# Attention of block 1 spread over the second pair of QKV quads, its regroup and output projection moved into the next FFN1

## The chip, the cores and the metric

The kernel runs on one core of a Trainium2 chip. The core has a matrix engine (TensorE, PE in the profile), three engines that work on vectors (VectorE or DVE, ScalarE or ACT, GpSimd or POOL), a queue engine (SyncE, SP), and 16 DMA engines that are fed from queues of SP, ACT and POOL. Each engine runs its own instructions strictly in the order in which the program lists them; an instruction that waits holds up all behind it on its engine. The metric is the device time of one execution in microseconds.

## The reference

The input x has 2048 tokens of 576 channels. It is normalised per token, and two branches are added to it:

```
xn  = layernorm(x)
q, k, v = split(xn @ wqkv)          # 32 heads of 18 channels
A: for token t: the 8 keys at t, t-2, ..., t-14 (those before token 0 are masked)
   o[t] = sum_w softmax_w(q[t].k[t-2w] / sqrt(18)) v[t-2w];   A = o @ wo
B: h = relu(xn @ w1 + b1) ** 2      # 576 -> 4608
   B = h @ w2 + b2                  # 4608 -> 576
out = x + A + B
```

## The kernel before

The tokens are worked on in four blocks of 512 (b = 0..3), two blocks making a half s. All products run on PE with operands split into a high and a low part of type fp32r, three partial products for each. ACT makes the high part (an activation), DVE the low part (a subtraction). So each weight tile costs PE its matmuls, ACT one instruction and DVE one, ahead of time: `w2_hi`/`w2_lo` split the FFN2 and projection weights two tiles ahead in the order of the list `stream`, in three buffers `w2s`; a buffer is loaded from memory three tiles ahead (`load_w2`, issued at the end of `w2_lo`).

The stages follow one another on PE:

1. q0: QKV of blocks 0 and 1, row by row.
2. `phase_a(0)`: FFN1 of blocks 0 and 1 in 18 pairs of hidden tiles (`ffn_pair`, a Strassen-like scheme over 2 x 2 parts, lines 524 to 649), with FFN2 of block 0 and then its output projection filled in between; the hidden tiles of block 1 go to memory.
3. `phase_b0` (945): FFN2 of block 1 in 36 steps n, then QKV of blocks 2 and 3 in four units of 14 quad steps each (`quad_step`, 890), then the output projection of block 1.
4. `phase_a(1)`: FFN1 of blocks 2 and 3, with FFN2 and the projection of block 2.
5. `phase_b1` (1094): FFN2 and the projection of block 3 in 34 + 5 steps, and `tail`.

The quads also follow a Strassen-like scheme. There are two pairs of units: k = 0 makes the channel groups 0 and 1, k = 1 the groups 2 and 3; half = 0, 1 are the two units of a pair. A unit has the steps (s, i) in the order (1,0) (1,1) (2,0) (2,1) (3,0) (3,1) (5,0) (4,0) (5,1) (4,1) (7,0) (6,0) (7,1) (6,1); s names the product, i one of two sets of four PSUM banks. This text counts the units 0 to 3 and the steps of a unit n = 0 to 13. Steps 0 to 5 have 6 matmuls each, steps 6 to 13 have 8. Steps with s = 4 to 7 send a row of results away through `row` (908): ACT copies the bank into one of four buffers `st` and, for s = 4 and 6, DVE adds a second bank (line 95, `st<-p,st`). Step (6,i) accumulates in the bank that the add of step (4,i) reads. After each step `hook` (986) issues work for other stages, mostly the splitting of weights.

Attention does not use PE. A block has four groups of heads (order 3, 2, 1, 0 for block 1). `attention(b, g)` (361) is a generator: up to each `yield` it issues one piece, and a group has 18 pieces: for j = 0..3 a product of queries with shifted keys (`pr<-q,kv`) and a reduction (`lg<-pr`); one piece with the maximum, its subtraction and the exponential on ACT (`lg<-lg`, line 380); one with the sum, reciprocal and scaling; for j = 0..3 a product with the values (`pr<-lg,kv`) and a tree of three additions (`pr<-pr` twice, `q<-pr`). After the last piece POOL issues 8 DMAs of the result to memory (`o<-q`, 400).

`side(k)` issues the next k pieces from the queue of groups; called with False it stops in front of a piece marked "exp". `complete(b)` issues all that is left of the blocks up to b at once. Keys and values have three buffers `kv`; `free` counts the free ones, `release` (348) gives one back and calls `fetch` (332), which loads the next keys or values on POOL's DMA queue. `regroup(1, .)` (706) takes such a buffer as well, and reads block 1's attention output back in two DMAs (`kv<-o`, 713). `o_hi(b, c)` and `o_lo(b, c)` (724, 743) transpose a fifth of it on DVE and split it (ACT, DVE) for the output projection `add(b, o_ops(b, c))`; the last one (c = 4) gives the buffer back.

Before the change `hook` calls `complete(1)` and `regroup(1, 0)` after the last step of unit 1 and then offers two groups of block 2. During units 2 and 3 pieces of group (2, 0) are issued, `o_hi` and `o_lo` for c = 0..3 follow steps 8 and 13 of unit 3, the projection parts c = 0, 1, 2 stand between the quads and FFN1, and c = 3, 4 are issued by `filler` inside the first pair of FFN1 at its places 0 and 1 (`work(0)`, `work(1)`). Temporary tiles of the name "r4" come from a pool of four buffers (`four`, 114).

Of the kernel before, what the change touches and what calls it, by code (L numbers as in the profile page):

```python
# [21 lines left out]
NJ = TB // P  # L22
# [23 lines left out]
def block_kernel(ctx: ExitStack, tc: tile.TileContext, x, xt, wqkv, wo, w1, b1, w2, b2, out):  # L46
# [280 lines left out]
        a = t[:, j:j + 1, 0:1]  # L327
        return bass.AP(tensor=a.tensor, offset=a.offset, ap=[a.ap[0], [DIL * CG, W], *dims])

    loads, landed, queue, free, lane, held = [], {}, [], [0], [nc.sync], [False]  # L330

    def fetch():
        while free[0] and loads and not held[0]:
            free[0] -= 1
            kind, b, g = loads.pop(0)
            if kind == "x":
                load_rows(b)
                landed["x", b] = True
                continue
            t = landed[kind, b, g] = sb.tile([P, NE, CG], F32, name="kv", bufs=3)  # L340
            if kind == "k":
                q = landed["q", b, g] = sb.tile([P, NJ, CG], F32, name="q", bufs=2)
                lane[0].dma_start(q.rearrange("p j c -> p (j c)"),
                                  flat(scr["q"][g], (PAD + b * TB) * CG, [NJ * CG, P], NJ * CG))
            lane[0].dma_start(t.rearrange("p e c -> p (e c)"),
                              flat(scr[kind][g], (PAD + b * TB - HALO) * CG, [NJ * CG, P], NE * CG))
# [14 lines left out]
    def attention(b, g):  # L361
        k, q = landed.pop(("k", b, g)), landed.pop(("q", b, g))
        lg = sb.tile([P, NA, W], F32, name="lg")
        mx = sb.tile([P, NA], F32, name="mx")
        sm = sb.tile([P, NA], F32, name="sm")
        for j in range(NJ):
            pr = sb.tile([P, W, CG], F32, name="pr")
            tt(pr, q[:, j:j + 1].to_broadcast([P, W, CG]), shifted(k, j, [1, CG]), ALU.mult)
            if j == NJ - 1:
                release()  # L370
            yield
            nc.vector.tensor_reduce(out=lg[:, j * HG:(j + 1) * HG].rearrange("p a w -> p w a"),  # L372
                                    in_=pr.rearrange("p w (a d) -> p w a d", d=DH), axis=AX.X, op=ALU.add)
            yield "exp" if j == NJ - 1 else None
        if b == 0:
            l4 = lg[:4].rearrange("p (j h) w -> p j h w", j=NJ)
            tt(l4, l4, mask[:4, :, None].to_broadcast([4, NJ, HG, W]), ALU.add)
        nc.vector.tensor_reduce(out=mx, in_=lg, axis=AX.X, op=ALU.max)
        tt(lg, lg, mx[:, :, None].to_broadcast([P, NA, W]), ALU.subtract)
        nc.scalar.activation(lg, lg, AF.Exp, scale=SCALE)  # L380
        yield
        nc.vector.tensor_reduce(out=sm, in_=lg, axis=AX.X, op=ALU.add)
        nc.vector.reciprocal(sm, sm)
        tt(lg, lg, sm[:, :, None].to_broadcast([P, NA, W]), ALU.mult)
        yield
        v = landed.pop(("v", b, g))
        for j in range(NJ):
            pr = sb.tile([P, W, CG], F32, name="pr")
            at = lg[:, j * HG:(j + 1) * HG].rearrange("p a w -> p w a")
            tt(pr.rearrange("p w (a d) -> p w a d", d=DH), at[:, :, :, None].to_broadcast([P, W, HG, DH]),  # L390
               shifted(v, j, [DH, HG], [1, DH]), ALU.mult)
            yield
            tt(pr[:, :4], pr[:, :4], pr[:, 4:], ALU.add)
            tt(pr[:, :2], pr[:, :2], pr[:, 2:4], ALU.add)
            tt(q[:, j], pr[:, 0], pr[:, 1], ALU.add)
            if j == NJ - 1:
                for k, (a, z) in enumerate(OPART):
                    rows = oscr[b, k][g * L:(g + 1) * L].rearrange("l (j i) c -> l i j c", i=G)
                    for i in range(G):
                        nc.gpsimd.dma_start(rows[:, i], q[i * L:(i + 1) * L, :, a:z])  # L400
                release()
            yield
# [3 lines left out]
    def side(k, exp=True):  # L406
# [13 lines left out]
                current[0] = None  # L420
        return 0

    def complete(b):
        while (any(n[0] == "k" and n[1] <= b for n, _ in queue)
               or current[0] is not None and current[2][0] == "k" and current[2][1] <= b):
            left = side(1)
            assert not left or current[0] is None

# [95 lines left out]
    def ffn_pair(s, p, work, first=False):  # L524
# [55 lines left out]
        if not last:  # L580
            combine_w1(n + 1)
        if not first:
            side(1 if p == 1 else 2 + p % 2, False)
        work(0)
        product(bb, T2, ss(2))
        w2_hi()
# [119 lines left out]
    def regroup(b, k):  # L706
        if b == 1:
            assert free[0]
            free[0] -= 1
            t = sb.tile([P, NJ * G * CG], F32, name="kv", bufs=3)  # L710
            for i, n in enumerate((OA, OB)):
                ob[b, i] = t[:, i * NJ * G * OA:][:, :NJ * G * n].rearrange("p (r c) -> p r c", c=n)
# [232 lines left out]
    def phase_b0():  # L945
# [6 lines left out]
        for n in range(NF):  # L952
# [7 lines left out]
            if n % 2 and n // 2 + 3 < NP:  # L960
                load_h(0, n // 2 + 3)
            if n < 33:
                run(pieces, 1 + n % 2)
            if n == 3:
                load_xt(3)
            if n == 33:
# [19 lines left out]
        def hook(k, half, s, i):  # L986
# [9 lines left out]
            if half and not k:  # L996
# [32 lines left out]
                if (s, i) == (6, 1):  # L1029
                    split_side(1, 1)  # L1030
                    split_slot(B22, b22)
                    complete(1)
                    regroup(b, 0)
                    for g in (0, 1):
                        offer(2, g)
            if at == (1, 0, 2, 1):
# [2 lines left out]
            if half and k:  # L1039
# [3 lines left out]
                    w1_hi(NP, 0)  # L1043
                    w1_lo(NP, 0)
                if (s, i) == (5, 1):
                    o_hi(b, 0), o_hi(b, 1)
                    o_lo(b, 0), o_lo(b, 1)
                if (s, i) == (4, 1):
                    w1_hi(NP, 1)
                    w1_lo(NP, 1)  # L1050
                if (s, i) == (6, 1):
                    o_hi(b, 2), o_hi(b, 3)
                    o_lo(b, 2), o_lo(b, 3)

        for k in range(2):
            for half in range(2):
                for s, i in ((1, 0), (1, 1), (2, 0), (2, 1), (3, 0), (3, 1), (5, 0), (4, 0), (5, 1), (4, 1),
                             (7, 0), (6, 0), (7, 1), (6, 1)):
                    quad_step(k, s, 2 * half + i, i)
                    hook(k, half, s, i)  # L1060
                    if (s, i) in ((2, 0), (2, 1), (3, 0), (5, 0), (5, 1), (4, 1), (7, 0), (7, 1)) and (k, half) != (0, 1):
                        side(1, s == 7)
                    if (s, i) in ((2, 1), (5, 0), (7, 0)) and (k, half) == (0, 1):
                        side(1, s == 7)
        for g in (2, 3):
            offer(2, g)
        for g in range(G):
# [1 line left out]
        xr[b] = [mt.tile([P, NC - 1, TB], F32, name="h", bufs=3)]  # L1069
        nc.sync.dma_start(xr[b][0], yscr)  # L1070
        open_y(b)
        for c in range(3):
            w2_hi()
            add(b, o_ops(b, c))
            w2_lo()
            if c == 0:
                o_hi(b, 4)
                o_lo(b, 4)
                open_left(b)
                nc.sync.dma_start(kept(b, NC - 1), yleft)  # L1080

        def filler(i):
            if i < 2:
                add(b, o_ops(b, 3 + i), range(NC) if i else ())
            if i == 1:
                finish(b, False)

        return filler
# [5 lines left out]
    def phase_b1():  # L1094
        b = 3
        open_y(b)
        for n in range(NF - 2):
# [6 lines left out]
                h_lo(1, n // 2 + 1)  # L1104
            if n % 2 and n // 2 + 3 < NP:
                load_h(1, n // 2 + 3)
            if b not in xr and (n == 22 or not queue and current[0] is None):
                complete(b)
                regroup(b, 0)
                regroup(b, 1)  # L1110
                residual(b)
                open_left(b)
                load_left(b)
            if n in range(27, 27 + NC):
                o_hi(b, n - 27)
                o_lo(b, n - 27)
            side(1 + n % 2)
        for c in range(NC):
            w2_hi()
# [349 lines left out]
```

## Time and profile before

| | us |
|---|---|
| median of 3 runs (1156.4 to 1159.25) | 1158.44 |
| the profiled execution | 1157.82 |
| its span from the first to the last instruction | 1156.1 |
| PE busy in the span | 1105.7 (96%) |
| DVE busy | 938.3 (81%) |
| ACT busy | 588.2 (51%) |
| POOL busy | 117.5 (10%) |

The page gives for each engine the time in which it executed something, and cuts the span into 40 slices of 28.9 us, with a digit for the busy share of each. A group of rows of the form "line engine op out<-in" names what is written and read by the names of the program's tiles. "[3.06 <-ACT w2s]" behind a row is idle time of the engine ahead of it and what ended it. In the view by windows the numbers behind the stretch are its length, and the busy time of PE, of PE's weight loads, of DVE, ACT and POOL with the number of instructions, then the clock granted to PE (1.00 is full), the busy share of the DMA engines, and GB/s.

### The profile page before, as it was taken

How to read it: one execution, taken by the hardware profiler on the slowest of the kernel's cores; microseconds unless marked ns; L12 is line 12 of the kernel's file. 1: busy time of each engine (PE TensorE's matmuls, PEld its weight loads, DVE VectorE, ACT ScalarE, POOL GpSimd, SP SyncE). 2: the span in 40 equal slices, each digit the busy share in tenths (PEclk: the TensorE clock that was granted, in tenths of full speed). 3: DMA queues.
4: the chain of work that ended last, by engine and by line, in shares of the span. 5: the costliest groups of instructions: out<-in, count | busy, mean ns of one | idle time of the engine just before them, and what ended most of it. 6: DMA issues, size and time to landing. Idle time of an engine off the chain costs nothing.

```text
span 1156.1 us, 13845 instructions
## 1 busy us (share of the span) xinstructions
PE 1105.7 (96%) x4966; PEld 931.0 (81%) x4966; DVE 938.3 (81%) x1238; ACT 588.2 (51%) x823; POOL 117.5 (10%) x219
## 2 busy tenths in 40 slices
PE   9999999999999999999944699999999999999998
PEld 7998888888888888888943588888888888888887
DVE  6697979897978779987795559998989898889864
ACT  5335566566656554554421137566565655543441
POOL 4000201030210200010012000210101020201100
PEclk9999999999999999999977799999999999999999
DMA  8954635475482758677733564625445453775672
GB/s 286 340 175 138 199 127 175 146 155 211 159 211 86 291 191 287 214 241 240 231 111 94 184 200 150 238 95 211 157 166 176 142 201 126 241 233 186 204 268 87
DMA packets 89558, 218.87 MB, mean 189 GB/s; under 512 B 12040, under 2 KB 40464, under 8 KB 83984
## 3 DMA queue, kind: packets, MB, share of 16 engines
q1 hardware_dynamic: 59456, 154.85, 39.6%
q0 software_dynamic: 10544, 52.14, 14.3%
q10 hardware_dynamic: 19488, 10.99, 3.2%
q8 instruction: 39, 0.64, 0.2%
q14 instruction: 31, 0.25, 0.1%
HBM read 174.21 MB, written 43.73 MB: 189 GB/s over the span
## 4 chain that ended last, share of the span: by engine, by line
PE 91%; DVE 5%; DMA 1%; issue 1%; ACT 1%; POOL 0%; ACTq 0%; POOLq 0%; DVEq 0%
PE p L513 45%; PE p L544 29%; PE p L548 5%; PE p L323 5%; PE p L902 5%; DVE pr L95 2%; PE p L1253 1%; PE p L906 1%; DMA kv<-kvq 1%; DVE lg L372 1%; DMA kv<-in_x 0%; DVE w1s L95 0%; POOL o L400 0%; DVE r L95 0%; PE p L1215 0%
## 5 line engine op out<-in xcount | busy, mean ns | idle before, releaser
L513 PE MATMUL p<-h,w2s 128*128 128x512 f32 x2066 | 493.2, 390 | 0.3 <-ACT h L555 0.2
L513 PEld LDWEIGHTS p<-h,w2s 128*128 128x128 f32 x2066 | 387.2, 188 | 83.6 <-ACT h L555 1.0
L544 PE MATMUL p<-X,w1s 128*128 128x512 f32 x864 | 219.5, 389 | 0.4 <-DVE w1s L95 0.4
L544 PEld LDWEIGHTS p<-X,w1s 128*128 128x128 f32 x864 | 162.1, 188 | 34.3 <-DVE w1s L95 0.8
L486 ACT ACTIVATE w2s<-w2r 128x640 fp32r<-128x640 f32 x164 | 120.5, 735 | 128.4 <-PE p L513 97.9
L544 PE MATMUL p<-S,w1s 128*128 128x512 f32 x648 | 164.5, 389 | 0.0
L95 DVE TENSOR_TENSOR w2s<-w2r,w2s 128x576 fp32r<-128x576 f32 x164 | 123.5, 754 | 43.1 <-ACT w2s L486 42.6
L544 PEld LDWEIGHTS p<-S,w1s 128*128 128x128 f32 x648 | 121.6, 188 | 25.3
L400 POOL DMA_DIRECT2D o<-q x128 | 69.1, 605 | 676.6 <-DVE q L95 674.7
L95 DVE TENSOR_TENSOR w1s<-w1r,w1s 128x1024 fp32r<-128x1024 f32 (+1 forms) x78 | 94.3, 1209 | 25.6 <-ACT w1s L459 25.4
L551 ACT ACTIVATE r<-r,b1t 128x512 f32<-128x512 f32 x72 | 52.0, 722 | 109.0 <-DVE r L95 109.0
L95 DVE TENSOR_TENSOR pr<-q,kv 128x1152 f32<-128x1152 f32 x64 | 86.8, 1357 | 17.9 <-DMA kv<-kvq 16.3
L95 DVE TENSOR_TENSOR pr<-lg,kv 128x1152 f32<-128x1152 f32 x64 | 86.6, 1354 | 0.8
L372 DVE TENSOR_REDUCE lg<-pr 128x64 f32<-128x1152 f32 x64 | 86.4, 1350 | 0.9
L95 DVE TENSOR_TENSOR h<-r,h 128x1024 fp32r<-128x1024 f32 (+3 forms) x46 | 51.8, 1137 | 36.5 <-ACT r L559 29.1
L95 DVE TENSOR_TENSOR pr<-pr 128x576 f32<-128x576 f32 (+1 forms) x128 | 77.6, 607 | 3.5
L459 ACT ACTIVATE w1s<-w1r 128x1024 fp32r<-128x1024 f32 x72 | 75.7, 1052 | 4.1 <-PE p L902 1.8
L559 ACT ACTIVATE r<-r 128x1024 f32<-128x1024 f32 x72 | 75.5, 1051 | 0.1
L95 DVE TENSOR_TENSOR w1r<-w1r 128x256 f32<-128x256 f32 (+3 forms) x118 | 66.2, 561 | 2.7
L548 PE MATMUL p<-x,w1s 128*128 128x512 f32 x216 | 66.5, 389 | 0.0
L95 DVE TENSOR_TENSOR r<-p,r 128x512 f32<-128x512 f32 (+1 forms) x77 | 52.9, 687 | 11.8 <-ACT r L609 8.5
L588 ACT ACTIVATE r<-p 128x512 f32<-128x512 f32 x36 | 21.6, 599 | 71.2 <-PE p L544 71.2
(172 smaller groups left out, 1115.5 us busy)
## 6 DMA issues: line engine op xcount, KB each, us to landing
w2r<-in_w SPq DMA_DIRECT2D x144, 320.0 KB, 3.3
kv<-kvq POOLq DMA_DIRECT2D x29, 1296.0 KB, 7.1
w1r<-in_w SPq DMA_DIRECT2D x36, 640.0 KB, 4.5
h<-r SPq DMA_DIRECT2D x36, 512.0 KB, 3.3
h<-h SPq DMA_DIRECT2D x36, 512.0 KB, 4.3
kvq<-st ACTq DMA_DIRECT2D x48, 216.0 KB, 3.1
w2r<-in_wo SPq DMA_DIRECT2D x20, 320.0 KB, 3.0
w1r<-in_xt SPq DMA_DIRECT2D x6, 1024.0 KB, 8.5
```

Source lines behind the costliest of these rows:

```text
L95: return nc.vector.tensor_tensor(out=out, in0=a, in1=b, op=op)
L323: nc.tensor.matmul(p[:, :QW], l, r, start=k == 0, stop=k == len(mm) - 1)
L372: nc.vector.tensor_reduce(out=lg[:, j * HG:(j + 1) * HG].rearrange("p a w -> p w a"), in_=pr.rearrange("p w (a d) -> p w a d", d=DH), axis ...
L400: nc.gpsimd.dma_start(rows[:, i], q[i * L:(i + 1) * L, :, a:z])
L459: nc.scalar.activation(w1s[n, k][:, 0], raw1[n][:, 4 * k:4 * k + 4], AF.Copy)
L486: nc.scalar.activation(w2s[stream[i]][:, :DE], raw2[i], AF.Copy)
L513: nc.tensor.matmul(yp[b][c], v, a, start=c not in yb[b], stop=c in last and c not in [o[0] for o in ops[i + 1:]], skip_group_check=True)
L544: nc.tensor.matmul(to, l, r, start=start and i == 0, stop=i == len(mm) - 1, skip_group_check=True)
L548: nc.tensor.matmul(to, weight(LEFT, k, f), v, start=False, stop=k == 1, skip_group_check=True)
L551: nc.scalar.activation(to, a, AF.Relu, bias=b1t[:, f:f + 1])
L559: nc.scalar.activation(r, r, AF.Square)
L902: nc.tensor.matmul(to, l[:, js], r, start=start and n == 0, stop=n == len(mm) - 1, skip_group_check=True)
```

## The change

- `complete(1)` and `regroup(1, 0)` no longer follow unit 1. Pieces of block 1's attention are issued one at a time behind chosen quad steps: steps 2, 3, 4, 8, 10, 12 of unit 0; 3, 6, 10, 12 of unit 1; 1 to 12 of unit 2; 3, 6, 8, 10 of unit 3. What is left is issued by `complete(1)` after step 8 of unit 3, and the regroup follows as soon as nothing of block 1 is left (`due`).
- From the end of unit 1 until the regroup `kept_back` is 1: `fetch` leaves one `kv` buffer free for the regroup.
- `o_hi`, `o_lo` for c = 0, 1 move from step 8 of unit 3 to its step 12. No projection part stands ahead of FFN1 now: c = 0, 1 with `o_hi(4)` are issued at place 0 of its first pair, c = 2, 3, 4 and `finish` at place 1. The tile of `open_left` is taken from "r4" ahead of that of `o_hi(1, 4)`.
- The mark "exp" now stands behind the maximum and subtraction; the exponential shares a piece with the sum.
- In the last eleven steps (n = 22 to 32) of block 1's FFN2 that call `run`, it issues two pieces each, not one and two in turn.
- In FFN1 of blocks 2 and 3 the first call of `side` in a pair asks for 2 + (p % 3 > 0) pieces in place of 2 + p % 2; in `phase_b1` the completion of block 3's attention is due by step 25 in place of 22, and `o_hi`, `o_lo` stand behind steps 29 to 33 in place of 27 to 31.

```diff
@@ -327,10 +327,10 @@
         a = t[:, j:j + 1, 0:1]
         return bass.AP(tensor=a.tensor, offset=a.offset, ap=[a.ap[0], [DIL * CG, W], *dims])
 
-    loads, landed, queue, free, lane, held = [], {}, [], [0], [nc.sync], [False]
+    loads, landed, queue, free, lane, kept_back = [], {}, [], [0], [nc.sync], [0]
 
     def fetch():
-        while free[0] and loads and not held[0]:
+        while free[0] > kept_back[0] and loads:
             free[0] -= 1
             kind, b, g = loads.pop(0)
             if kind == "x":
@@ -371,14 +371,14 @@
             yield
             nc.vector.tensor_reduce(out=lg[:, j * HG:(j + 1) * HG].rearrange("p a w -> p w a"),
                                     in_=pr.rearrange("p w (a d) -> p w a d", d=DH), axis=AX.X, op=ALU.add)
-            yield "exp" if j == NJ - 1 else None
+            yield
         if b == 0:
             l4 = lg[:4].rearrange("p (j h) w -> p j h w", j=NJ)
             tt(l4, l4, mask[:4, :, None].to_broadcast([4, NJ, HG, W]), ALU.add)
         nc.vector.tensor_reduce(out=mx, in_=lg, axis=AX.X, op=ALU.max)
         tt(lg, lg, mx[:, :, None].to_broadcast([P, NA, W]), ALU.subtract)
+        yield "exp"
         nc.scalar.activation(lg, lg, AF.Exp, scale=SCALE)
-        yield
         nc.vector.tensor_reduce(out=sm, in_=lg, axis=AX.X, op=ALU.add)
         nc.vector.reciprocal(sm, sm)
         tt(lg, lg, sm[:, :, None].to_broadcast([P, NA, W]), ALU.mult)
@@ -420,9 +420,12 @@
                 current[0] = None
         return 0
 
+    def due(b):
+        return (any(n[0] == "k" and n[1] <= b for n, _ in queue)
+                or current[0] is not None and current[2][0] == "k" and current[2][1] <= b)
+
     def complete(b):
-        while (any(n[0] == "k" and n[1] <= b for n, _ in queue)
-               or current[0] is not None and current[2][0] == "k" and current[2][1] <= b):
+        while due(b):
             left = side(1)
             assert not left or current[0] is None
 
@@ -580,7 +583,7 @@
         if not last:
             combine_w1(n + 1)
         if not first:
-            side(1 if p == 1 else 2 + p % 2, False)
+            side(1 if p == 1 else 2 + (p % 3 > 0 if s else p % 2), False)
         work(0)
         product(bb, T2, ss(2))
         w2_hi()
@@ -707,6 +710,7 @@
         if b == 1:
             assert free[0]
             free[0] -= 1
+            kept_back[0] = 0
             t = sb.tile([P, NJ * G * CG], F32, name="kv", bufs=3)
             for i, n in enumerate((OA, OB)):
                 ob[b, i] = t[:, i * NJ * G * OA:][:, :NJ * G * n].rearrange("p (r c) -> p r c", c=n)
@@ -960,7 +964,7 @@
             if n % 2 and n // 2 + 3 < NP:
                 load_h(0, n // 2 + 3)
             if n < 33:
-                run(pieces, 1 + n % 2)
+                    run(pieces, 2 if n > 21 else 1 + n % 2)
             if n == 3:
                 load_xt(3)
             if n == 33:
@@ -1029,8 +1033,7 @@
                 if (s, i) == (6, 1):
                     split_side(1, 1)
                     split_slot(B22, b22)
-                    complete(1)
-                    regroup(b, 0)
+                    kept_back[0] = 1
                     for g in (0, 1):
                         offer(2, g)
             if at == (1, 0, 2, 1):
@@ -1043,25 +1046,28 @@
                     w1_hi(NP, 0)
                     w1_lo(NP, 0)
                 if (s, i) == (5, 1):
-                    o_hi(b, 0), o_hi(b, 1)
-                    o_lo(b, 0), o_lo(b, 1)
+                    complete(1)
                 if (s, i) == (4, 1):
                     w1_hi(NP, 1)
                     w1_lo(NP, 1)
+                if (s, i) == (7, 1):
+                    o_hi(b, 0), o_hi(b, 1)
+                    o_lo(b, 0), o_lo(b, 1)
                 if (s, i) == (6, 1):
                     o_hi(b, 2), o_hi(b, 3)
                     o_lo(b, 2), o_lo(b, 3)
-
+            if kept_back[0] and not due(1):
+                regroup(b, 0)
+                fetch()
+
+        steps = [(1, 0), (1, 1), (2, 0), (2, 1), (3, 0), (3, 1), (5, 0), (4, 0), (5, 1), (4, 1), (7, 0), (6, 0), (7, 1), (6, 1)]
         for k in range(2):
             for half in range(2):
-                for s, i in ((1, 0), (1, 1), (2, 0), (2, 1), (3, 0), (3, 1), (5, 0), (4, 0), (5, 1), (4, 1),
-                             (7, 0), (6, 0), (7, 1), (6, 1)):
+                for n, (s, i) in enumerate(steps):
                     quad_step(k, s, 2 * half + i, i)
+                    if n in ((2, 3, 4, 8, 10, 12), (3, 6, 10, 12), range(1, 13), (3, 6, 8, 10))[2 * k + half]:
+                        side(1)
                     hook(k, half, s, i)
-                    if (s, i) in ((2, 0), (2, 1), (3, 0), (5, 0), (5, 1), (4, 1), (7, 0), (7, 1)) and (k, half) != (0, 1):
-                        side(1, s == 7)
-                    if (s, i) in ((2, 1), (5, 0), (7, 0)) and (k, half) == (0, 1):
-                        side(1, s == 7)
         for g in (2, 3):
             offer(2, g)
         for g in range(G):
@@ -1069,20 +1075,23 @@
         xr[b] = [mt.tile([P, NC - 1, TB], F32, name="h", bufs=3)]
         nc.sync.dma_start(xr[b][0], yscr)
         open_y(b)
-        for c in range(3):
-            w2_hi()
-            add(b, o_ops(b, c))
-            w2_lo()
-            if c == 0:
+        open_left(b)
+        nc.sync.dma_start(kept(b, NC - 1), yleft)
+
+        def filler(i):
+            if i == 0:
+                for c in range(2):
+                    w2_hi()
+                    add(b, o_ops(b, c))
+                    w2_lo()
                 o_hi(b, 4)
                 o_lo(b, 4)
-                open_left(b)
-                nc.sync.dma_start(kept(b, NC - 1), yleft)
-
-        def filler(i):
-            if i < 2:
-                add(b, o_ops(b, 3 + i), range(NC) if i else ())
             if i == 1:
+                add(b, o_ops(b, 2))
+                w2_hi()
+                w2_lo()
+                add(b, o_ops(b, 3))
+                add(b, o_ops(b, 4), range(NC))
                 finish(b, False)
 
         return filler
@@ -1104,16 +1113,16 @@
                 h_lo(1, n // 2 + 1)
             if n % 2 and n // 2 + 3 < NP:
                 load_h(1, n // 2 + 3)
-            if b not in xr and (n == 22 or not queue and current[0] is None):
+            if b not in xr and (n == 25 or not queue and current[0] is None):
                 complete(b)
                 regroup(b, 0)
                 regroup(b, 1)
                 residual(b)
                 open_left(b)
                 load_left(b)
-            if n in range(27, 27 + NC):
-                o_hi(b, n - 27)
-                o_lo(b, n - 27)
+            if n in range(29, 29 + NC):
+                o_hi(b, n - 29)
+                o_lo(b, n - 29)
             side(1 + n % 2)
         for c in range(NC):
             w2_hi()
```

## The prediction

> **What bounds the kernel now.** I read the page's slices first, then the stretch where PE is not full by windows, then the waits and the order of time there. PE sets the time:
>
> ```profile
> PE   9999999999999999999944699999999999999998
> ```
>
> It is full except in slices 21 to 23, the quads. By windows (units 0 and 1, the first hole, the start of unit 2, the second hole, the restart; busy time of PE, its weight loads, DVE, ACT, POOL):
>
> ```profile
> 547.80:567.40 19.60, 19.60 (x101) 18.83 (x101) 15.64 (x19) 7.73 (x14) 0.54 (x1) 1.00 0.82 262
> 567.40:586.80 19.40, 19.40 (x101) 18.66 (x101) 16.26 (x22) 10.66 (x18) 0.00 (x0) 1.00 0.46 141
> 586.80:611.50 24.70, 4.80 (x26) 4.31 (x24) 22.91 (x28) 3.60 (x8) 4.33 (x8) 0.64 0.30 92
> 611.50:623.00 11.50, 11.50 (x52) 10.82 (x52) 10.98 (x16) 3.50 (x7) 0.00 (x0) 0.88 0.13 39
> 623.00:646.80 23.80, 0.22 (x2) 0.00 (x0) 7.31 (x9) 0.53 (x1) 7.52 (x14) 0.61 0.59 208
> 646.80:654.10 7.30, 7.29 (x25) 6.81 (x26) 6.14 (x6) 1.07 (x2) 0.53 (x1) 0.65 0.40 117
> ```
>
> Two holes, each followed by a stretch at a low clock: (1 - 0.88) x 11.5 = 1.4 us and (1 - 0.65) x 7.3 = 2.6 us. The waits of that stretch name the holes:
>
> ```profile
> PE p L902 <- DVE st L95: 23.6, 1, 23.6
> PEld p L902 <- ACT p L920: 20.2, 1, 20.2
> PE p L902 <- ACT p L920: 19.9, 1, 19.9
> ```
>
> The first hole (19.9) is `complete(1)`: VectorE works off 23 pieces, and ScalarE, whose exponential stands in that row, holds the copy (920) that PE needs. In order of time: unit 1's last split, the first key and value pieces of (1,0), its last addition, and the result's way through memory:
>
> ```profile
> 589.91 1.05 DVE L95 TENSOR_TENSOR h<-w1r,h 128x864 fp32r<-128x864 f32 x1
> ...
> 598.54 1.36 DVE L95 TENSOR_TENSOR pr<-q,kv 128x1152 f32<-128x1152 f32 x1
> ...
> 612.34 1.36 DVE L95 TENSOR_TENSOR pr<-lg,kv 128x1152 f32<-128x1152 f32 x1
> ...
> 624.08 0.31 DVE L95 TENSOR_TENSOR q<-pr 128x144 f32<-128x144 f32 x1
> 624.68 4.31 POOL L400 DMA_DIRECT2D o<-q  x8 [21.54 <-DVE q L95]
> 628.78 0.76 POOL L713 DMA_DIRECT2D kv<-o  x1
> ```
>
> The second hole (23.6) follows: the keys of (2,0) are loaded only behind the regroup, VectorE stands in front of them, and the row add of unit 2 stands behind it. The chain shows what the quads lose:
>
> ```profile
> 547.80 8.22 PE p L902 x42
> ...
> 631.84 8.79 DMA kv<-kvq
> ...
> 673.68 0.54 ACT st L911
> ```
>
> A matmul takes 8.22 / 42 = 0.196 us, so a unit of 100 takes 19.6 and four 78.3. From 547.8 to 673.7 pass 125.9 us: **47.5 us lost**.
>
> **The change part by part.** The sum goes against the profiled execution's 1157.8 us, 0.6 below the median of the runs.
>
> *Both holes go: -47.5.* Counting pieces in the code's order, 28 of block 1 remain when the quads begin (34 before: the six extra pieces in its FFN2). Units 0 and 1 issue 10 (before 11), unit 2 12, unit 3 the last 6. A group's ten key and softmax pieces take 612.34 - 598.54 = 13.8 us, its eight value pieces 624.4 - 612.34 = 12.1, or 3.0 per pair. Unit 2 gets 7 key pieces (9.7 us), both softmax pieces (2.7) and 3 value pieces (4.4), with four row adds of 0.6: 19.2 us of VectorE in 19.6 of PE. It fits. VectorE enters about 4 us late (the split above ends at 591.0, unit 2 starts at 547.8 + 2 x 19.6 = 587.0) and leaves about 3 late. The add of step (4,i) has three more steps, some 4.7 us, until (6,i) needs its bank, so I cost this at 0, and at 4 if VectorE runs that much later. In unit 0 and 1 DVE has 15.6 and 16.3 of 19.6, as now.
>
> *The six extra pieces in block 1's FFN2: 0.* By my count of its instructions VectorE gets 3 to 4 us behind in n = 30 to 32, less than the two tiles (6.3 us) by which weights are split ahead, and it can catch up in the last steps:
>
> ```profile
> 540.00:547.80 7.80, 7.80 (x36) 6.48 (x35) 3.37 (x6) 2.30 (x3) 0.00 (x0) 1.00 0.73 248
> ```
>
> Bounds 0 and 2.
>
> *A new stall between quads and FFN1: +8.0.* In unit 3 VectorE starts 3 us late, does (durations of these shapes as in the quads of the trace) the w1 combination (1.6), a tree (1.6), a split (1.2), a product (1.4), waits for the row of (4,0) until 10.8, adds it (0.5), then tree, product, tree: block 1's attention ends 15.9 us into the unit. From there the way through memory is to be bounded (a regroup in the FFN phases, this one, an output row; the last number is us from issue to landing):
>
> ```profile
> st<-o POOLq DMA_DIRECT2D x3, 768.0 KB, 11.0
> ...
> kv<-o POOLq DMA_DIRECT2D x1, 768.0 KB, 5.0
> ...
> out<-r SPq DMA_DIRECT2D x4, 128.0 KB, 2.5
> ```
>
> The attention ended at 624.4; the regroup's first part (c = 0 to 2) was issued 4.4 us later and landed at 633.8, 9.4 behind the end. Now `release` issues the values of (2,0) on POOL's queue ahead of the regroup. By their tiles values or keys have 1296 KB, the regroup's second part 384, queries 288; between the landing of the first part and that of the keys (631.84 + 8.79 = 640.6) the queue moved 384 + 288 + 1296 KB in 6.8 us, so the values can cost the regroup up to 6.8 x 1296 / 1968 = 4.5 us. R, its landing counted from the start of unit 3, is between 15.9 + 9.4 = 25.3 and 29.8. I take 28.4, nearer the upper end, since in the trace what was issued later on this queue landed later. The Trainium skill, DMA: Bandwidth & Descriptors, section "Two DMAs through the same engine are not ordered", says that the descriptors of one queue start in order. By that rule R is 29.8 and the sum 1.4 us longer; it speaks against this change, and the trace agrees in that the keys landed behind the regroup.
>
> What waits: `o_hi(1, 0)` and `(1, 1)` after step 12 hold DVE, and their copies ACT. Behind them stand the copy and add of row (6,1), which free banks 7 and 1 for the projection. PE ends unit 3 at 19.6, runs two products and a matmul of FFN1 (3.0, to 22.6) and stops at the projection. Transposes, copies, splits and the add end at R + 3.1; four matmuls (0.9) fit before. Stall: R + 3.1 - 0.9 - 22.6 = R - 20.4 = 8.0, bounds 4.9 and 9.4. Afterwards VectorE (12 us of splits, transposes and flips by R + 11.5) stays ahead of PE, which needs the last of them at R + 16.
>
> *The clock: +1.9.* PE stopped at 586.8 + 4.8 = 591.6, and
>
> ```profile
> 594.00:596.00 2.00, 0.00 (x0) 0.00 (x0) 1.90 (x4) 0.00 (x0) 0.00 (x0) 0.50 0.56 230
> ```
>
> so 8 us of idleness are enough for the half clock; its price lies between the 1.4 and 2.6 above.
>
> *A buffer of "r4": +1.1.* With four buffers in turn, taking `open_left`'s tile ahead of `o_hi(4)`'s makes the first pair's `r1` the successor of that tile, which is free only when the last output row has gone out. Before:
>
> ```profile
> 692.77 2.49 DVE L95 TENSOR_TENSOR h<-p,h 128x512 f32<-128x512 f32 x4 [9.00 <-PE p L513]
> ...
> 696.60 0.49 SPq L790 DMA_DIRECT2D out<-r  x1
> ...
> 698.73 1.52 PE L544 MATMUL p<-X,w1s 128*128 128x512 f32 x6
> ```
>
> The output lands at 696.6 + 2.5 = 699.1, the add into `r1` (0.7) then ends at 699.8, and the product at 698.73 needs it: 1.1 us; 0 if buffers are not given out in turn. The 9.0 us in which VectorE waits for PE there cover all else that moves into the first pair.
>
> *FFN1 of blocks 2 and 3: 0.* Fifteen pieces of group (2,0) move out of the quads into it, but the new numbers of pieces again make 18 per three pairs (counted with the halts at "exp"), so VectorE's load stays:
>
> ```profile
> 1023.30:1090.00 66.70, 66.70 (x295) 54.93 (x294) 64.73 (x85) 26.26 (x35) 4.35 (x8) 1.00 0.59 192
> 842.50:895.50 53.00, 53.00 (x235) 43.89 (x235) 46.52 (x60) 31.77 (x43) 5.96 (x11) 1.00 0.50 166
> ```
>
> The second row is three pairs: 46.5 of 53.0 us.
>
> *Block 3's FFN2: +4.0.* The first row is this stage, where VectorE has 97%. The delayed pieces end up here: in the count attention ends at step 19 now, and after the change four pieces are left at step 25 and issued at once (6.0 us). VectorE is already late there, as ScalarE's copy and VectorE's split of step 19 show:
>
> ```profile
> 1083.60 0.74 ACT L486 ACTIVATE w2s<-w2r 128x640 fp32r<-128x640 f32 x1 [1.48 <-PE p L513]
> ```
>
> ```profile
> 1088.50 0.75 DVE L95 TENSOR_TENSOR w2s<-w2r,w2s 128x576 fp32r<-128x576 f32 x1
> ```
>
> The copy ends at 1084.3, the split starts 4.2 us later, and at 97% VectorE doesn't catch up: I take 4.7 at step 25. A step has 14 matmuls of 66.7 / 295 = 0.226, 3.17 us; with the four pieces and a split (0.7) the lag is 4.7 + 6.0 + 0.7 - 3.2 = 8.2 at step 26. Weights split in step n are used 0.9 us into step n + 2, so up to 6.35 + 0.9 - 1.5 = 5.75 is bearable: PE loses 2.45. Then the regroup of block 3. The attention ends 12.1 us behind the start of step 25 (lag, split and pieces), the transposes come with step 29, at 12.7. By the rows above the landing is 4.4 + 5.0 = 9.4 to 4.4 + 11.0 = 15.4 us behind the end; with 11 VectorE stands until 23 us, and PE loses another 1.5 by step 33. Bounds: 0 (3 us less lag, 9.4) and 8 (15.4).
>
> Sum: 1157.8 - 47.5 + 8.0 + 1.9 + 1.1 + 4.0 = **1125 us**.
>
> **Rivals.**
> *Almost all is hidden* (0.14): R is 25.3, no buffer waits, block 3's steps absorb their pieces; 4.9 + 1.4 is left: 1117. For it speak the 4.5 us between bounds; against it VectorE's 97%.
> *VectorE is late everywhere* (0.19): unit 2 or 3 slips by 4 us, block 3's regroup takes 15.4 us (8 in place of 4) and PE's waits there halve its clock for a while (2.6): 1125 + 10.6 = 1136. For: units 2 and 3 leave VectorE under 1 us each.
> *The holes only move* (0.03): if the pieces are not issued as counted, `complete(1)` behind step 8 of unit 3 (11.7 us) issues all 18 (25.9): R is 11.7 + 25.9 + 12.5 = 50.1, the stall R - 20.4 = 29.7 in place of 8.0: 1147. Against: nothing keeps (1,0)'s keys away.
> *Slower: FFN1 of blocks 2 and 3 becomes VectorE's* (0.08). One mechanism: pairs with seven pieces follow each other (p % 3 = 1, 2) and each makes PE wait. It must cost the 32.8 us gained over 17 pairs, 1.9 us per pair, before the change is slower; three pairs would need 53.0 + 5.7 us of VectorE, where they have 46.5. At 2.2 per pair it ends at 1162; a quarter of its chance lies between 1.7 and 2.1, where no change would show.
>
> **Numbers.** The forecast, 1125, has 0.56, its own range 1119 to 1132. The range from 1115 to 1139 takes in the first two rivals. Those below 1155 are the faster ones. The runs agree within about 0.3%, which is what can be told from no change. Faster 0.92, same 0.02, slower 0.06.
>
> **What would show it.** Steps 2 to 13 of units 2 and 3 without waits on `st`; one idle time of PE of 5 to 9 us in front of the first projection matmul, ended by DVE or ACT behind `kv<-o`, with the half clock; VectorE idle in front of `r<-p,r` in the first pair until `out<-r` has landed; PE waits of 2 to 4 us for `w2s` near step 28 of block 3. It would be wrong if PE waited in unit 2, or if VectorE's share in FFN1 rose above 95%.

## The result and the profile after

| | before | after |
|---|---|---|
| median of 4 runs, us | 1158.01 (1156.4 to 1159.25) | 1139.77 (1135.06 to 1140.19) |
| the profiled execution, us | 1157.82 | 1140.19 |
| its span, us | 1156.1 | 1138.5 |

The kernel is faster by 1.7%: after to before is 0.983, with a 95% interval from 0.9805 to 0.9863. By the two spans it gained 17.6 us, where 32.8 were forecast. The median lies 0.8 us above the forecast range of 1115 to 1139; by the ratio, 0.9834 x 1157.8 = 1138.6, the time is at the upper edge of that range.

The page of the kernel after, its busy times and the slices of PE and of PE's clock:

```profile
PE 1110.8 (98%) x4966; PEld 932.9 (82%) x4966; DVE 935.4 (82%) x1238; ACT 586.5 (52%) x823; POOL 116.0 (10%) x219
...
PE   9999999999999999999899699999999999999978
...
PEclk9999999999999999999999899999999999999989
```

The two slices of 4 in the quads are gone. What is left are an 8 (the end of block 1's FFN2 and unit 0), a 6 (between quads and FFN1) and, new, a 7 near the end, where PE was full before.

By windows, kernel after (columns as in the prediction): the last steps of block 1's FFN2, units 0 to 3, the start of FFN1, FFN1 of blocks 2 and 3, and the end of block 3's FFN2:

```profile
540.00:547.90 7.90, 7.90 (x37) 6.54 (x36) 6.77 (x9) 2.29 (x3) 0.54 (x1) 1.00 0.74 274
547.90:573.40 25.50, 21.50 (x102) 20.22 (x101) 14.33 (x22) 7.47 (x14) 0.00 (x0) 0.93 0.76 242
573.40:593.00 19.60, 19.60 (x102) 18.67 (x101) 16.36 (x22) 10.04 (x18) 0.59 (x2) 1.00 0.31 92
593.00:612.60 19.60, 19.60 (x102) 18.84 (x101) 19.26 (x24) 8.85 (x17) 4.85 (x9) 1.00 0.82 256
612.60:632.10 19.50, 19.50 (x101) 18.55 (x100) 17.41 (x26) 8.30 (x14) 3.31 (x7) 1.00 0.34 97
632.10:650.00 17.90, 9.24 (x30) 6.58 (x30) 8.43 (x15) 4.10 (x8) 3.19 (x6) 0.71 0.82 284
650.00:990.00 340.00, 339.67 (x1497) 280.51 (x1496) 285.12 (x363) 199.12 (x270) 31.97 (x59) 1.00 0.49 172
1083.00:1112.00 29.00, 21.29 (x76) 16.78 (x75) 15.56 (x21) 7.86 (x11) 5.38 (x10) 0.82 0.59 198
```

Units 1, 2 and 3 are full at the full clock. Three stretches are not: unit 0 takes 25.5 us in place of 19.6, the stretch behind unit 3 has PE busy 9.2 of 17.9 us, and block 3's FFN2 loses 7.7 of 29.0 us. The waits of PE in the kernel after (us in total, times, the longest) put names to them:

```profile
PE p L516 <- ACT h L738: 8.7, 1, 8.7
...
PE p L516 <- ACT h L803: 4.7, 1, 4.7
...
PE p L906 <- DVE h L783: 4.0, 1, 4.0
...
PE p L516 <- DVE w2s L95: 3.0, 1, 3.0
```

The 4.0 is at the start of unit 0 (line 783 adds the residual into block 1's output). The 8.7 is the projection of block 1. The 3.0 and the 4.7 are both in block 3. How much had been gained where is read from the chain, kernel after (start, us, what):

```profile
544.98 7.33 DMA h<-in_xt
...
633.65 8.84 DMA kv<-o
...
670.12 2.72 PE p L547 x12
```

and the chain of the kernel before, the same group of FFN1 as the last row above:

```profile
700.71 2.72 PE p L544 x12
```

So behind the quads the kernel is 700.71 - 670.12 = 30.6 us ahead, and at the end 17.6. With 47.5 us of holes gone, 16.9 were given back between 547.9 and 670, and 13.0 in block 3's FFN2. Unit 0 accounts for 25.5 - 19.6 = 5.9, or 6.0 by its unrounded ends, of the 16.9; the other 10.9, by subtraction, are the stall behind unit 3.

Where these come from is seen in order of time. First SP's queue and VectorE in the kernel after, around the start of unit 0 (start, us over all that the row groups, engine and line, what it does):

```profile
537.25 7.63 SPq L479 DMA_DIRECT2D w2r<-in_wo  x3
543.78 1.42 DVE L95 TENSOR_TENSOR w2s<-w2r,w2s 128x576 fp32r<-128x576 f32 x2
544.98 1.09 SPq L769 DMA_DIRECT2D h<-in_xt  x1
552.41 2.73 DVE L783 SCALAR_TENSOR_TENSOR h<-p,b2t,h 128x512 f32<-128x512 f32 x4 [5.57 <-DMA h<-in_xt]
```

and in the kernel before:

```profile
539.27 0.75 DVE L95 TENSOR_TENSOR w2s<-w2r,w2s 128x576 fp32r<-128x576 f32 x1
540.47 0.38 SPq L765 DMA_DIRECT2D h<-in_xt  x1
```

The residual of block 1 (`h<-in_xt`) is issued 4.5 us later. The same three weight loads (`w2r<-in_wo`) stand ahead of it in both kernels. The last of them fills a buffer that a split on VectorE (`w2s<-w2r,w2s`) must have read before, and that split, the first of the two in its row, starts at 543.78 in place of 539.27, also 4.5 us later. The residual lands at 544.98 + 7.33 = 552.3, after unit 0 has begun, and VectorE has waited 5.6 us for it. Then the end of the quads, kernel after, with block 1's last piece, its way through memory and the first projection matmul:

```profile
628.19 0.31 DVE L95 TENSOR_TENSOR q<-pr 128x144 f32<-128x144 f32 x1
628.79 4.33 POOL L400 DMA_DIRECT2D o<-q  x8 [28.67 <-DVE q L95]
632.91 0.76 POOL L345 DMA_DIRECT2D kv<-kvq  x1
633.65 0.57 POOL L717 DMA_DIRECT2D kv<-o  x1
638.10 0.55 POOL L717 DMA_DIRECT2D kv<-o  x1 [3.89 <-issue]
642.51 1.30 DVE L737 STREAM_TRANSPOSE r<-kv 128x512 f32<-128x512 f32 x2 [9.19 <-DMA kv<-o]
643.93 9.11 PE L516 MATMUL p<-h,w2s 128*128 128x512 f32 x28 [8.66 <-ACT h L738]
```

And block 3's FFN2, kernel after:

```profile
1085.22 0.31 DVE L95 TENSOR_TENSOR q<-pr 128x144 f32<-128x144 f32 x1
...
1086.26 13.47 PE L516 MATMUL p<-h,w2s 128*128 128x512 f32 x52 [3.01 <-DVE w2s L95]
...
1093.57 0.56 POOL L724 DMA_DIRECT2D st<-o  x1 [3.14 <-DMA o<-q]
...
1101.42 0.71 DVE L737 STREAM_TRANSPOSE r<-st 128x512 f32<-128x512 f32 x1 [9.64 <-DMA st<-o]
...
1104.43 7.80 PE L516 MATMUL p<-h,w2s 128*128 128x512 f32 x22 [4.70 <-ACT h L803]
```

The attention of block 3 ends at 1085.5, so late that its pieces first starve PE of weights (3.0), and its regroup lands 15.9 us later, with VectorE standing in front of the transposes for 9.6 us and PE for 4.7.

### The profile page after: what moved, and what is told of

The parts are those of the page before. It is cut to its first block, busy times and chain, and to the rows that moved or that the text cites. A ratio compares the mean times of both kernels' runs of the same rounds, so it can differ in the third digit from the quotient of the medians.

```text
span 1138.5 us, 13845 instructions
## 1 busy us (share of the span) xinstructions
PE 1110.8 (98%) x4966; PEld 932.9 (82%) x4966; DVE 935.4 (82%) x1238; ACT 586.5 (52%) x823; POOL 116.0 (10%) x219
## 4 chain that ended last, share of the span: by engine, by line
PE 77%; DVE 11%; DMA 5%; issue 3%; ACT 2%; POOL 1%; ACTq 0%; DVEq 0%; SPq 0%; POOLq 0%
PE p L516 35%; PE p L547 28%; PE p L551 5%; PE p L906 5%; DVE pr L95 3%; DVE h L95 2%; DVE lg L372 1%; PE p L323 1%; DVE w2s L95 1%; DMA kvq<-st 1%; PE p L910 1%; DMA kv<-o 1%; DMA w2r<-in_w 1%; DMA kv<-kvq 1%; DMA st<-o 1%
## 5 line engine op out<-in xcount | busy, mean ns | idle before, releaser
L516 PE MATMUL p<-h,w2s 128*128 128x512 f32 x2066 | 500.1, 393 | 17.3 <-ACT h L738 8.7
```

What stands on the lines that cost most here:

```text
L516: nc.tensor.matmul(yp[b][c], v, a, start=c not in yb[b], stop=c in last and c not in [o[0] for o in ops[i + 1:]], skip_group_check=True)
```

## The experiments

The theory after the result: three separate places give back the 16.9 + 13.0 = 30 us: (a) six extra pieces in block 1's FFN2 push the residual back on SP's queue; (b) the values of (2,0) go ahead of the regroup on POOL's queue; (c) the halts at the mark "exp" in FFN1 push pieces of block 3 to its end. The rivals differ from place to place and stand with each run. Diffs are against the kernel after. The runs were made in two groups; the median of the kernel before was 1156.15 us beside the first four kernels and 1157.53 beside the other four, so kernels are compared by their ratios to it or by spans.

**The residual issued one step earlier.**

```diff
@@ phase_b0, in the loop over n
             add(b, tile_products(b, n, hs[0, n // 2]), range(NC) if n == NF - 1 else ())
+            if n == 32:
+                residual(b)
+                xr[b].append(sb.tile([P, TB], F32, name="xf"))
+                load_left(b)
             w2_lo()
...
             if n == 33:
                 run_all(pieces)
                 defer[0] = False
-                residual(b)
-                xr[b].append(sb.tile([P, TB], F32, name="xf"))
-                load_left(b)
```

> The changed kernel with the load of block 1's residual issued one step earlier, ahead of step 32's weight load on SP's queue. Theory: in the changed kernel this load (issued at 545.0 us, landing 7.3 us later) makes VectorE's drain wait until 552.4 and PE wait 4.0 us in unit 0, with a slow clock behind it; unit 0 takes 25.6 us instead of 19.6. So unit 0 comes back to about 19.6 us and the time falls by 6, to about 1134. Rival: the drain is late because VectorE itself is behind from the six extra pieces; then unit 0 still takes about 25 us and the time stays at 1140.

Measured: 1131.03 us (1130.24 to 1133.61), ratio 0.978 (0.9766 to 0.9803), span 1129.5. By the ratio that is 0.005 x 1156 = 5.8 us better than the kernel after, by the profiled spans 9.0. SP's queue in this kernel, and its unit 0 by windows:

```profile
537.19 0.33 SPq L479 DMA_DIRECT2D w2r<-in_wo  x1
537.57 0.42 SPq L769 DMA_DIRECT2D h<-in_xt  x1
```

```profile
547.97:567.55 19.58, 19.58 (x101) 18.80 (x101) 13.80 (x22) 7.62 (x14) 0.00 (x0) 1.00 0.83 269
```

What follows: the load now stands ahead of the weight loads of steps 32 and 33 and leaves at 537.6, unit 0 is full, and PE's wait for line 783 is gone, with the six extra pieces still in place. It was the place in SP's queue, not VectorE's load itself. Some 3 us of the profiled gain lie elsewhere (the wait of 4.7 in block 3 is 3.4 here); they are less than the 5 us by which executions of the kernel after differ.

**No halts at "exp" in FFN1 of blocks 2 and 3.**

```diff
-            side(1 if p == 1 else 2 + (p % 3 > 0 if s else p % 2), False)
+            side(1 if p == 1 else 2 + (p % 3 > 0 if s else p % 2), s == 1)
...
-        side(2, False)
+        side(2, s == 1)
```

> The changed kernel with the halt in front of the exponential left out in FFN1 of blocks 2 and 3, so that no piece is lost there. Counted in the code's order, block 3's attention then ends at step 18 of its FFN2 (step 25 in the changed kernel, 19 before). Theory: the 13 us that the changed kernel loses in block 3's FFN2 come from the four pieces at step 25 and the regroup behind them; both go, and the time falls by 12 to 13, to about 1127. Rival: FFN1 can't bear the pieces (exponential on ScalarE in front of the copies PE needs); then waits of PE of several us in all appear in FFN1 and eat most of it, 1135 or more.

Measured: 1132.89 us (1128.46 to 1134.04), ratio 0.979 (0.9767 to 0.9811); the profiled execution is the fastest of the four, with a span of 1126.8, 11.7 below the kernel after. By windows, the end of block 3's FFN2 in this kernel:

```profile
1070.00:1110.00 40.00, 40.00 (x178) 33.14 (x177) 22.82 (x29) 17.23 (x23) 0.27 (x1) 1.00 0.62 200
```

What follows: both waits of block 3 and the low clock behind them are gone, so they came from the pieces that FFN1 had not taken; and FFN1 can take them, at the price of waits of 1.7 us in all (for `r`, line 547). The whole time missed the expected 1127: by the ratio the gain is 0.0045 x 1156 = 5.2 us, where 12 to 13 were expected, since the other three runs, 1132.3 to 1134.0, gained less than the profiled one. Its wait at unit 0 was 2.8 us, where the kernel after has 4.0 and other kernels with the late residual 4.5 and 5.0; that this wait differs from run to run is likely a part of it, but the other runs left no profile, and it stays open.

**The regroup ahead of the values on POOL's queue.**

```diff
@@ hook
+            if at == (1, 1, 1, 0):
+                kept_back[0] = 2
```

> The changed kernel with block 1's regroup issued ahead of the values of group (2,0) on POOL's queue. Theory: the values cost the regroup 4.6 us (it landed 14.0 us behind the attention's end, 9.4 before the change), so PE's wait in front of the projection falls from 8.7 to about 4, and the time by 4 to 6, to about 1135. Rival: the regroup waits for its own stores (8 DMAs) and the order doesn't matter: wait 8 or more, time 1139 to 1140.

Measured: 1136.3 us (1131.87 to 1138.39), ratio 0.982 (0.9796 to 0.9845), span 1136.7. In order of time, this kernel's last piece, the regroup, and the first projection matmul (the values are issued at 642.32 here):

```profile
631.67 0.31 DVE L95 TENSOR_TENSOR q<-pr 128x144 f32<-128x144 f32 x1
...
637.20 0.56 POOL L717 DMA_DIRECT2D kv<-o  x1 [0.59 <-DMA o<-q]
...
644.26 7.97 PE L516 MATMUL p<-h,w2s 128*128 128x512 f32 x23 [5.50 <-ACT h L738]
```

What follows: without 1296 KB ahead of it the regroup takes 5.6 us from issue to landing in place of 8.8 (its row in the chain is `637.20 5.61`), it lands 10.8 us behind the attention's end in place of 14.0, and PE waits 5.5 in place of 8.7. The mechanism is as thought and smaller: the values cost 3.2 us, not 4.6, since the way through memory takes 10.8 us even without them, where 9.4 had been read from the kernel before. The gain in the whole time, 1.6 us by the ratio and 1.8 by the spans, lies inside the overlap of the two intervals and was not resolved here.

**Block 3's regroup without its wait for the attention.** The projection of block 3 reads the output of block 2.

```diff
@@ regroup
-        nc.gpsimd.dma_start(t.rearrange("p r c -> p (r c)"), oscr[b, k].rearrange("p r c -> p (r c)"))
+        nc.gpsimd.dma_start(t.rearrange("p r c -> p (r c)"), oscr[b if b < 3 else 2, k].rearrange("p r c -> p (r c)"))
...
-                complete(b)
...
+                complete(b)
```

> The changed kernel with block 3's regroup issued ahead of its last four pieces and reading block 2's attention output, which has long been in memory; block 3's projection so uses block 2's attention. Theory: of the 13 us lost in block 3's FFN2, PE's wait of 4.7 us for the regroup and the slow clock behind it (2.8) go, the wait of 3.0 us for the weights at step 28 and its slow clock (1.7) stay: about 1132. Rival: the four pieces alone set the loss (VectorE's lag only shows up twice): time 1139 to 1140.

Measured: 1134.56 us (1134.4 to 1136.28), ratio 0.981 (0.9799 to 0.9828), span 1132.8, 5.7 below the kernel after. The one wait of PE that this kernel has between 1060 and 1120:

```profile
PE p L516 <- DVE w2s L95: 2.5, 1, 2.5
```

What follows: the 4.7 was the regroup's way through memory, as the prediction had it in kind; the wait for weights stays, so it comes from the pieces and not from the regroup. The two are separate terms. The gain of 5.7 us is less than the 7.5 expected; PE's waits at unit 0 and in front of block 1's projection are 1.2 us longer here (4.5 and 9.4 us, 4.0 and 8.7 in the kernel after).

**All three edits together.**

> The changed kernel with the residual's load one step earlier, no halt at the exponential in FFN1 of blocks 2 and 3, and block 1's regroup ahead of the values, all three together. Theory: the three losses stand in different stages, so the gains add: 6 + 12 + 4 less than the changed kernel's span of 1138.5, about 1116; PE is left with one wait of 4 to 5.5 us in front of the projection. Rival: they share a resource (VectorE or the DMA engines) and give some of it back: 1120 or more.

Measured: 1120.69 us (1119.91 to 1121.28), ratio 0.968 (0.9664 to 0.9693), span 1119.5. By the ratio the three give 0.0156 x 1157 = 18 us on top of the change, by the spans 19.0. Alone they gave 9.0 + 11.7 + 1.8 = 22.5 by the spans and 5.8 + 5.2 + 1.6 = 12.6 by the ratios. The time is at the bound set for the rival (1120 or more); the span is 3.5 above the expected 1116. PE's waits in this kernel between FFN2 of block 1 and the end of block 3:

```profile
PE p L516 <- ACT h L738: 5.6, 1, 5.6
...
PE p L547 <- DVE r L95: 1.5, 1, 1.5
```

What follows: the three causes together account for 18 to 19 of the 30 us that the change gave back, and the waits aimed at are gone or shorter, as in the runs one by one. Whether the gains add in full is not shown: the joint gain lies between the two sums, and a small loss to a shared resource is not excluded. The 5.6 is what the regroup costs even without the values ahead of it.

**Without the six extra pieces.**

```diff
-                    run(pieces, 2 if n > 21 else 1 + n % 2)
+                    run(pieces, 1 + n % 2)
```

> The changed kernel without the six extra pieces in block 1's FFN2 (one part undone). Theory: VectorE is on time there, so the residual's load is issued as before the change and unit 0 takes 19.6 us again (-6); but eight pieces are left behind step 8 of unit 3, the attention ends about 9 us later in it, and PE's wait in front of the projection grows from 8.7 to 17 or more (+9): span about 1141. Rival: the late residual has nothing to do with the extra pieces: unit 0 stays at 25 us.

Measured, one execution: 1144.67 us, span 1143.0, 4.5 above the kernel after. Its two largest waits of PE:

```profile
PE p L906 <- DVE st L95: 10.5, 1, 10.5
...
PE p L516 <- ACT h L738: 6.5, 1, 6.5
```

What follows: unit 0 is full again (19.58 us, from 548.86 to 568.44), a second sign that these pieces delayed the residual. But they have to go somewhere: left to the end of unit 3 they cost 17.0 us where the stall had cost 8.7. How that splits was a miss: 10.5 of it is the row add behind `complete(1)`, inside the unit, and not in front of the projection. By these waits (8.3 us more, against 6.0) taking six pieces early was worth more than it cost; the whole time of a single execution can't show it.

**Pieces moved from unit 3 to unit 0**, on top of the three edits:

```diff
-                    if n in ((2, 3, 4, 8, 10, 12), (3, 6, 10, 12), range(1, 13), (3, 6, 8, 10))[2 * k + half]:
+                    if n in ((2, 3, 4, 7, 8, 9, 10, 11, 12), (3, 6, 10, 12), range(1, 13), (1, 2, 3, 4, 8, 10))[2 * k + half]:
```

> The three edits together, and three more pieces in unit 0 (steps 2, 3, 4, 7 to 12), so that block 1's attention ends behind step 2 of unit 3 instead of step 8. Theory: PE's wait in front of the projection is the attention's end plus the way through memory, so with an end some 6 to 8 us earlier the wait falls below 1 us and the time is 5 to 6 below that of the three edits, about 1110. Rival: VectorE has no room in unit 0 or 1, falls behind and makes PE wait for row adds in units 1 and 2: no gain over the three edits.

Measured: 1114.73 us (1113.67 to 1115.24), ratio 0.963 (0.9613 to 0.9645), span 1112.0. The page's slices of this kernel, its largest waits of PE behind the program's first matmuls, its unit 0 by windows, and the first DMA of block 1's last result:

```profile
PE   8999999999999999999999999999999999999998
...
PEclk9999999999999999999999999999999999999999
```

```profile
PE p L516 <- DVE h L95: 1.8, 2, 1.5
PE p L547 <- DVE r L95: 1.5, 1, 1.5
```

```profile
547.90:567.50 19.60, 19.60 (x102) 18.84 (x101) 16.33 (x26) 7.62 (x14) 0.00 (x0) 1.00 0.80 248
```

```profile
615.06 4.33 POOL L400 DMA_DIRECT2D o<-q  x8 [28.45 <-DVE q L95]
```

By the ratio that is 5.7 us below the three edits together; the expected 5 to 6 came, from a higher start, so that 1110 was not reached. What follows: unit 0 had room for three more pieces (VectorE is busy for 16.3 of 19.6 us there). Unit 3 starts at 606.7 in this kernel, so the attention ends some 8 us into it in place of 15.9; the regroup's way through memory lies beside the rest of unit 3, and the projection doesn't wait. This is the fastest of all versions run, some 43 us below the kernel before.

**Block 3's attention due at step 22 again, its transposes behind steps 27 to 31.**

```diff
-            if b not in xr and (n == 25 or not queue and current[0] is None):
+            if b not in xr and (n == 22 or not queue and current[0] is None):
...
-            if n in range(29, 29 + NC):
-                o_hi(b, n - 29)
-                o_lo(b, n - 29)
+            if n in range(27, 27 + NC):
+                o_hi(b, n - 27)
+                o_lo(b, n - 27)
```

> The changed kernel with block 3's attention due by step 22 and its transposes at steps 27 to 31, as before the change (one part undone). Theory: eight pieces (12 us) are then issued at once; VectorE's lag at step 23 is some 15 us where 5.75 are borne, so PE loses some 9 us at step 25 and more for the regroup: 3 to 6 us longer than the changed kernel, a span of 1141 to 1145. Rival: the later due step itself costs the time: shorter than 1138.

Measured, one execution: 1140.41 us, span 1138.7, the kernel after's within 0.2. In block 3's FFN2 PE waited once:

```profile
PE p L516 <- DVE w2s L95: 9.2, 1, 9.2
```

What follows: the span missed the expected 1141 to 1145. The wait for weights came as expected (9), the wait behind the regroup did not: while PE stood, the result went on through memory, and VectorE waited 4.1 us for it in place of 9.6. As far as one execution shows, the pieces left over cost about the same at either step, and the later due step of the change bought nothing by itself.

## Why the prediction was right and wrong

The direction and the main term were right, and the total was 15 us too low. Of the rivals none came as described: the landing of the regroup (29.9 us behind the start of unit 3) and the waits in block 3 exclude the one in which almost all is hidden, the full units 1 to 3 the one in which the holes only move. "VectorE is late everywhere" has the nearest time, 1136, but by luck: 4.0 of it is a slip in units 2 and 3 that did not come. Two terms failed by several us, the six extra pieces (0, measured 6.0) and block 3's FFN2 (4.0, measured 13.0). Term by term:

| term of the sum | forecast (bounds) | measured |
|---|---|---|
| both holes | -47.5 | -47.5 |
| six extra pieces in block 1's FFN2 | 0 (0 to 2) | +6.0 |
| stall between quads and FFN1, with its clock | 8.0 + 1.9 (4.9 to 9.4, 1.4 to 2.6) | +10.9 |
| a buffer of "r4" | +1.1 (0 to 1.1) | 0 |
| FFN1 of blocks 2 and 3 | 0 | 0 |
| block 3's FFN2 | +4.0 (0 to 8) | +13.0 |
| sum | -32.5 | -17.6 |

*Both holes.* Right, and in detail: units 1 to 3 take 19.5 to 19.6 us with no wait of PE for `st`, and block 1's attention ended at 628.50, 15.9 us behind the start of unit 3 (612.60), the number that the count of pieces gave. VectorE has 19.26 of 19.6 us in unit 2, where 19.2 were worked out.

*The six extra pieces: 0.* This step failed. It asked whether VectorE's lag would starve PE of weights, and it did not: PE is full from 540.0 to 547.9, with VectorE at 6.8 us in place of 3.4. But `w2_lo` also frees the buffer for which a weight load waits on SP's queue, and the residual stands behind that load. The prediction followed the lag along VectorE and PE and not along the queue that `w2_lo` feeds. Two runs show it, the one with the residual moved ahead and the one without the pieces.

*The stall.* Right in place and kind, within the bounds in size: PE waited 8.7 us, and the regroup's landing R was 642.5 - 612.6 = 29.9, where 28.4 was taken and 29.8 was the upper bound. The Trainium skill, DMA: Bandwidth & Descriptors, "Two DMAs through the same engine are not ordered", with its descriptors that start in order, had given 29.8, and the trace agrees with it: with the values behind the regroup the landing came 3.2 us sooner. That 29.8 fits so closely is luck in part: the way without the values was taken too short (9.4, measured 10.8) and the price of the values too high (4.5, measured 3.2). What is left behind the wait, 10.9 - 8.7 = 2.2, is put down to the clock, forecast 1.9.

*A buffer of "r4".* The step failed, in the direction left open. In the kernel after, the first row below groups the two additions of the output row (64x512) and, as the third, the one into `r1` (128x512). They follow each other without a gap, and the third starts at 666.0, just as the output is issued and so before it can have landed:

```profile
664.59 2.12 DVE L95 TENSOR_TENSOR r<-p,r 64x512 f32<-64x512 f32 x3
...
666.02 0.49 SPq L794 DMA_DIRECT2D out<-r  x1
```

*FFN1.* Right: VectorE has 285 of 340 us (84%), and PE is busy for 339.7. The rival in which FFN1 of blocks 2 and 3 becomes VectorE's fell with it.

*Block 3's FFN2: 4.0.* This term failed in its size: right in both mechanisms, too small by 9 us, and above its upper bound of 8. The wait for weights was forecast as 2.45 and measured as 3.0. The regroup was forecast to cost 1.5 with its landing 11 us behind the attention's end; it landed after 15.9, above the upper bound of 15.4, and cost 4.7. And no low clock was counted for these waits. It is most of the difference: 13.0 - 7.7 = 5.3 us are not in the waits, and 4.5 of these can be counted, since the 52 matmuls behind the first wait took 13.47 us where 52 x 0.226 = 11.8, and the 22 behind the second 7.80 where 5.0. The other 0.8 stays open. The rival "VectorE is late everywhere" had that clock.

## What to carry to other kernels

When an engine gets behind, follow what it frees as well as what it makes: here a load that waited for a buffer held back the residual behind it on its queue by 4.5 us, and a residual that is needed at a stage's border should stand ahead of the loads that wait. Work taken out of a full stage comes back where the next halt lets it pile up, so count the pieces to the end of the program, and price each new wait of the matrix engine with the low clock that can follow it (1.7 to 2.8 us here), short waits too.

## What was not expected of the hardware

The clock falls after shorter waits than the prediction had rows for. The kernel after, 2 us from each of two stretches behind waits of 3.0 and 4.7 us:

```profile
1086.00:1088.00 2.00, 1.75 (x4) 1.47 (x5) 2.00 (x4) 0.00 (x0) 1.97 (x4) 0.50 0.53 133
1106.00:1108.00 2.00, 2.00 (x6) 1.52 (x5) 1.30 (x3) 1.26 (x2) 0.00 (x0) 0.50 0.21 82
```

A wait of 3.0 us already brought the half clock (0.50), and the stretch at that clock cost 1.7 to 2.8 us more, about as much after a wait of 3 as after one of 9. Other runs show that shorter waits can do it, but not always: behind the 2.5 us in block 3 of the run whose projection reads block 2's output the clock was 0.50 from 1090 to 1092, while behind the 2.7 us in block 3 (in front of line 516) of the run without the six extra pieces it was 1.00 from 1110 to 1118. The Trainium skill, TensorE: Matmul & The Clock Gate, section "What's actually happening", puts the fall behind an idle window of about 3.4 us that runs freely. The traces agree in kind, in that about the same wait brings the fall in one run and not in another, but not in the length: waits of 2.5 to 3.0 us were enough here. Waits of 1.5 us, in the fastest version, left the clock at 9 (90% or more) in every slice.

One thing stays open: POOL stood for 3.89 us ahead of the regroup's second DMA (638.10 above), put down to "issue". In the run with the regroup ahead of the values the same place has 3.54 us, put down to the DMA `o<-q`, so it is likely the attention's last result on its way there too. No run was made to separate it.
